# Attention halves, a VectorE split and two stores set elsewhere in a fused linear-attention and FFN kernel

## The chip, the cores and the metric

The kernel runs on one core of one Trainium2 chip. The metric is the device time of one execution in microseconds (us), as the median of several runs.

## The reference

There are 8 batches with 8 heads of 64, and 576 positions in each. Linear attention without a mask is normalised over each head, laid out as 4608 rows of 512, and goes through a feed-forward layer of width 2048:

```python
kv = np.einsum('bhsd,bhse->bhde', k, v)
out = np.einsum('bhsd,bhde->bhse', q, kv)
rms = np.sqrt(np.mean(out * out, axis=-1, keepdims=True) + 1e-06)
x = (out / rms * g_norm).transpose(0, 2, 1, 3).reshape(B * S, H * D)
h = x @ w_in
g = h * (1.0 / (1.0 + np.exp(-h)))
return g @ w_out
```

All is float32. Each operand of a large product is split into a high and a low part, and a product is hi·lo + hi·hi + lo·hi.

## The kernel before

**Tiles.** The rows are 9 tiles of 512 tokens, t = 0 to 8, and the width is 16 blocks of 128, f = 0 to 15. A batch is 576 tokens, so batch 0 fills t=0 and leaves 64 tokens over (class `Rest`, from L390 on), which with most of batch 1 make t=1. Tiles 0 and 1 use plain products: one step is 24 matmuls of 128x256 into an `hp` bank (`products`, L511 through `halves`), a gate, and two steps later 24 matmuls into four `acc` banks (`project`). Tiles 2 to 8 use sums of weight blocks, kept in DRAM (`sums_in_dram`) and loaded again for each pair of blocks (`load_sums`, L676). From t=7 on (`OUT7`) `seven_step` does two blocks at a time.

**The order is written by hand.** Each engine runs its instructions in the order in which the program issues them. A step of t=0 issues:

1. the jobs listed as first for this step;
2. the split of one wo block and one wi block: upper half by a cast on ACT (L215), lower half by a subtraction on POOL (L216);
3. the bit operations of the wo block of this step on DVE (L201, L204, L207), and the magnitude of a wi block four steps ahead on ACT (L181) and POOL (L182);
4. the products of the step on PE ("hp6" in the prediction is that of step 6), and its gate: two activations on ACT (L530, L531) and a subtraction on POOL (L532);
5. the bit operations of a wi block on DVE and the magnitude of a wo block (ACT L181, POOL L182);
6. the jobs listed as mid, the project of the step two back, and the jobs listed as last.

`at_third(n, ...)` puts a job into step n // 3, as first, mid or last by n % 3.

**Batch 1** runs during t=0. `SECOND` (L32) has a row for each of the four pairs of heads: the thirds at which kv and q are split, the first half of out is made, the second half, then its sums and its x. A half (`mm_out`, L314 to L316) is three matmuls into a bank with the tag `at`, 256 columns wide the first time and 320 the second; "p1.0" in the prediction is the first half of pair 1. `copy_out` squares it (ACT L320) and copies it (ACT L321). In t=0 there is one such bank, so a half starts when the one before has been copied. `low_q` (DVE L302) makes the low part of q, `turn_sq` (DVE L325) transposes the squares.

**Buffers.** Five buffers with the tag `tmp` go round in order of allocation: the magnitudes of wi (`full`), the squares and their transpose (`sq`, `sqT`), the scaled rest (`xf`), the results (`ob`) and others. An instruction that writes one waits for the last reader of what was in it.

**The batch-0 rest** goes to x by `x_from`. With `fast` false: scale on ACT into `xf` (L460), cast on ACT (L461), subtraction on POOL (L462). With `fast` true: a scaled cast on ACT from the bank (L451), and scale and subtraction in one DVE operation from the bank (L452).

**Stores.** The results of tile 6 are copied to SBUF in the first two steps of t=7 (`empty`), and each leaves a store of 256 KB in `stores`; the table `between` says at which slot of `seven_step` they are issued. All DMAs of this part are issued by SP, into one queue.

Of the kernel before, what the change touches and what calls it, by code (L numbers as in the profile page):

```python
# [28 lines left out]

SECOND = (13, 17, 18, 20, 39), (17, 19, 21, 24, 40), (19, 22, 24, 27, 44), (22, 25, 28, 30, 41)  # L32


@with_exitstack
def linear_attention_rms_silu_ffn(
# [23 lines left out]
    B, NP, P, S = q.shape  # L60
# [3 lines left out]
    TN = 512  # L64
# [68 lines left out]
    x_second = const.tile([P, NP, 2, TN], F32R, name="x_second")  # L133
# [17 lines left out]
    def block(kind, f, dtype):  # L151
        return weights.tile([P, 2, NP * P], dtype, name=f"{kind}{f}", tag=f"{kind}{f}")
# [101 lines left out]
    class Pair:  # L254
# [101 lines left out]
        def to_tile(self, segment):  # L356
            a, e, t, o = segments(self.b)[segment]
            th, tl = (x_part(t, i, self.c)[:, o:o + e - a] for i in range(2))
            nc.scalar.copy(out=th, in_=self.o[:, a:e])
            nc.gpsimd.tensor_tensor(out=tl, in0=self.o[:, a:e], in1=th.bitcast(F32), op=ALU.subtract)  # L360
# [37 lines left out]
    class Rest:  # L398
# [20 lines left out]
                nc.tensor.transpose(out=self.x[:, w], in_=self.on[:, w], identity=ident)  # L419

        def to_tile(self):
            return x_from([x_second[:, :, a, 0:S - TN] for a in range(2)], self.x.rearrange("d (c n) -> d c n", n=64), False)

    slots = [f"{kind}{f}" for f in range(NF - 1, 0, -1) for kind in ("wo", "wi")]

# [20 lines left out]
    def x_from(tiles, ps, fast):  # L446

        th, tl = tiles
        if fast:
            return [  # L450
                lambda: nc.scalar.activation(out=th, in_=ps, func=AF.Copy, scale=gcol),  # L451
                lambda: nc.vector.scalar_tensor_tensor(  # L452
                    out=tl, in0=ps, scalar=gcol, in1=th.bitcast(F32), op0=ALU.mult, op1=ALU.subtract
                ),
            ]
        full = tmp.tile([P, S], F32, name="xf", tag="tmp")
        a, n = ps.shape[1:]
        full = full[:, :a * n].rearrange("d (a n) -> d a n", n=n)
        return [
            lambda: nc.scalar.activation(out=full, in_=ps, func=AF.Copy, scale=gcol),  # L460
            lambda: nc.scalar.copy(out=th, in_=full),  # L461
            lambda: nc.gpsimd.tensor_tensor(out=tl, in0=full, in1=th.bitcast(F32), op=ALU.subtract),  # L462
        ]
# [29 lines left out]
    def h_bank():  # L493
        return ps_h.tile([P, 512], F32, name="hp", tag="h")
# [51 lines left out]
    emptied, stores = [], []  # L546
# [464 lines left out]
    sevens, queue, between = [], [], {}  # L1011
    W7 = 12, 11, 11, 8

    def open_sevens():

        once["products"], once["seventh"] = h_bank(), h_bank()
        once["forms"] = block("wi", HF + 5, F32)
        once["partial"] = kvq.tile([P, S], F32, name="partial", tag="kvq")[:, :TN].rearrange("p (j n) -> p j n", n=H)
        sevens.extend(Half(h) for h in range(2))
        between.update({(n + 2, "II"): [lambda n=n: load_quarter(OUT7 + 1, n)] for n in range(4)})  # L1020
        for key in ((1, "II"), (1, "III")):
            between[key] = [lambda: stores.pop(0)()] * 2

    def open_gated():

# [4 lines left out]
    def load_quarter(t, n):  # L1030
        row, w = ((0, low), (0, high), (1, high), (1, low))[n]
        nc.sync.dma_start(out=quarter(row, w), in_=x_in_dram[t, row][:, :, w])
# [54 lines left out]
    def seven_step(t, i, groups):  # L1087
# [4 lines left out]
        if opening:  # L1092
            open_sevens()
# [128 lines left out]
    def at_third(n, *calls):  # L1222
        at((first_jobs, mid_jobs, last_jobs)[n % 3], n // 3, *calls)
# [12 lines left out]
    def plan(b, g):  # L1236
# [51 lines left out]
        for p in ps:  # L1288
            half = [lambda p=p, i=i: out_half(p, i) for i in range(2)]
            sums = lambda p=p: p.sum_sq(norms[0][:, p.c])  # L1290
            if b == 1:
                split_at, first_at, second_at, sums_at = SECOND[p.c][:4]
                at_third(split_at, p.split_kv, p.low_kv, p.split_q, p.low_q)
# [34 lines left out]
        for p in ps:  # L1328
            if b == 1:
                n = SECOND[p.c][4]  # L1330
                at_third(n, lambda p=p: p.spread(norms[1][:, p.c], 0), lambda p=p: p.scale(0))
# [6 lines left out]
    with tc.manual_schedule():  # L1338
# [5 lines left out]
        for item in ORDER.split():  # L1344
            kind, n = item.rstrip("0123456789"), int(item.lstrip("wiopbgq") or 0)
# [255 lines left out]
```

## Time and profile before

| what | value |
|---|---|
| runs | 800.72, 800.72, 812.23 us; median 800.72 |
| the profiled execution | 800.1 us, its span 798.3 us |
| granted TensorE clock | 0.998 |
| PE busy | 787.2 us (99%) |
| DVE, ACT, POOL busy | 611.7 (77%), 413.8 (52%), 112.4 us (14%) |
| DMA | 171.08 MB, mean 214 GB/s |

Rows of the timeline read: start, duration, engine, line, operation, out<-in with shapes, count, and in brackets the idle time of the engine before it with what released it. The waits read: engine, output and line that waited, what ended the wait, then total, times and longest in us. Ends of matmuls are modelled, since PE overlaps them; the start of the next matmul says more.

### The profile page before, as it was taken

The page shows a single profiled execution, that of the slowest core. Times are in us where ns is not written, and L with a number is a line of the kernel's source. Part 1 is how long each engine was busy: PE and PEld are TensorE (multiplying, and loading weights), DVE is VectorE, ACT ScalarE, POOL GpSimd, SP SyncE. Part 2 cuts the span into 40 slices and gives each one's busy share as a digit, 9 for nine tenths or more (in the row PEclk, how much of TensorE's full clock was granted, in tenths as well). Part 3 has the DMA queues.
Part 4 walks back from the last instruction along what each step waited for, and adds up shares of the span by engine and source line. Part 5 has one row for each costly group of instructions (what it writes and reads, how often), then busy time and mean ns, then how long its engine had stood idle before and what let it go on. Part 6 is the DMA issues. An engine that isn't in the chain of part 4 may idle for free.

```text
span 798.3 us, 18479 instructions
## 1 busy us (share of the span) xinstructions
PE 787.2 (99%) x7292; PEld 781.2 (98%) x7292; DVE 611.7 (77%) x1328; ACT 413.8 (52%) x871; POOL 112.4 (14%) x116
## 2 busy tenths in 40 slices
PE   8999999999999999999999999999999999999997
PEld 7899999999999999999999999999999999999997
DVE  4999956789779768769878677678867886788666
ACT  4888455445546445635645445445644654465443
POOL 2799781223000000000000000000000000000000
PEclk9999999999999999999999999999999999999999
DMA  9994012743666866766676436976687567657553
GB/s 343 413 413 148 4 61 80 244 157 136 224 236 200 290 218 200 253 215 232 227 256 225 165 107 220 329 250 211 217 252 227 200 225 254 209 201 225 198 186 119
DMA packets 74457, 171.08 MB, mean 214 GB/s; under 512 B 8322, under 2 KB 23170, under 8 KB 74370
## 3 DMA queue, kind: packets, MB, share of 16 engines
q1 hardware_dynamic: 74370, 169.90, 62.4%
q8 instruction: 57, 0.93, 0.5%
q14 instruction: 30, 0.25, 0.1%
HBM read 137.36 MB, written 32.51 MB: 213 GB/s over the span
## 4 chain that ended last, share of the span: by engine, by line
PE 91%; DMA 5%; POOL 2%; issue 1%; DVE 1%; ACT 0%; SPq 0%; DVEq 0%; POOLq 0%
PE hp L747 33%; PE acc L511 26%; PE acc L927 10%; PE hp L511 9%; PE at L927 5%; DMA wo<-in_moe_w_out 3%; PE hp L927 3%; PE at L277 2%; DMA early_wo<-in_q 1%; PE at L314 1%; PE at L315 1%; PE at L316 1%; DMA wi<-sums_in_dram 1%; POOL wo L216 1%; POOL gl L532 0%
## 5 line engine op out<-in xcount | busy, mean ns | idle before, releaser
L511 PE MATMUL acc<-wo,gh 128*128 128x256 f32 x1280 | 200.1, 276 | 0.3 <-POOL wo L216 0.3
L511 PEld LDWEIGHTS acc<-wo,gh 128*128 128x128 f32 x1280 | 170.5, 188 | 0.5 <-POOL wo L216 0.5
L747 PE MATMUL hp<-x_second,wi 128*128 128x256 f32 x1152 | 153.4, 277 | 0.0
L747 PEld LDWEIGHTS hp<-x_second,wi 128*128 128x128 f32 x1152 | 141.1, 188 | 0.3
L511 PE MATMUL acc<-wo,gl 128*128 128x256 f32 x640 | 124.6, 276 | 0.0
L747 PE MATMUL hp<-operand,wi 128*128 128x256 f32 x912 | 120.9, 276 | 0.6 <-DMA wi<-sums_in_dram 0.4
L747 PEld LDWEIGHTS hp<-operand,wi 128*128 128x128 f32 x912 | 111.3, 188 | 1.0 <-DMA wi<-sums_in_dram 0.6
L511 PEld LDWEIGHTS acc<-wo,gl 128*128 128x128 f32 x640 | 96.3, 188 | 0.0
L873 ACT ACTIVATE wi<-wi 128x512 f32<-128x512 f32 x64 | 40.5, 633 | 97.5 <-DVE wi L1181 75.0
L978 POOL TENSOR_TENSOR e<-e,partial 128x256 f32<-128x256 f32 x2 | 1.5, 733 | 592.3 <-DVE e L978 592.3
L927 PE MATMUL acc<-wo,gh 128*128 128x256 f32 x256 | 46.8, 276 | 0.0
L511 PE MATMUL hp<-x_second,wi 128*128 128x256 f32 x384 | 46.3, 277 | 0.0
L511 PE MATMUL hp<-x,wi 128*128 128x256 f32 x360 | 44.5, 278 | 0.7 <-POOL x L462 0.7
L511 PEld LDWEIGHTS hp<-x_second,wi 128*128 128x128 f32 x384 | 45.0, 188 | 0.1
L511 PEld LDWEIGHTS hp<-x,wi 128*128 128x128 f32 x360 | 42.4, 188 | 1.1 <-POOL x L462 0.9
L927 PE MATMUL acc<-s,gs 128*128 128x256 f32 x288 | 43.0, 276 | 0.0
L320 ACT ACTIVATE sq<-at 128x256 f32<-128x256 f32 (+1 forms) x56 | 22.9, 409 | 36.1 <-PE at L316 29.8
L1181 DVE TENSOR_TENSOR wi<-hp,partial 128x256 f32<-128x256 f32 x32 | 13.6, 425 | 35.9 <-PE hp L747 35.9
L927 PEld LDWEIGHTS acc<-wo,gh 128*128 128x128 f32 x256 | 38.6, 188 | 0.0
L927 PEld LDWEIGHTS acc<-s,gs 128*128 128x128 f32 x288 | 37.4, 188 | 0.0
L1166 ACT COPY wi<-hp 128x256 f32<-128x256 f32 x32 | 11.9, 373 | 48.4 <-PE hp L747 48.4
L747 PE MATMUL hp<-moved,wi 128*128 128x256 f32 x288 | 36.8, 277 | 0.0
(207 smaller groups left out, 1660.8 us busy)
## 6 DMA issues: line engine op xcount, KB each, us to landing
wi<-sums_in_dram SPq DMA_DIRECT2D x112, 512.0 KB, 3.8
s<-out_sums SPq DMA_DIRECT2D x96, 256.0 KB, 4.7
wi<-in_moe_w_in SPq DMA_DIRECT2D x16, 512.0 KB, 8.1
wo<-in_moe_w_out SPq DMA_DIRECT2D x16, 512.0 KB, 9.0
sums_in_dram<-sum_parts SPq DMA_DIRECT2D x16, 512.0 KB, 2.9
out_sums<-wi SPq DMA_DIRECT2D x16, 512.0 KB, 3.0
k<-in_k SPq DMA_DIRECT2D x28, 288.0 KB, 4.3
v<-in_v SPq DMA_DIRECT2D x28, 288.0 KB, 4.6
```

What stands on the lines that cost most here:

```text
L216: nc.gpsimd.tensor_tensor(out=w[:, 1, :], in0=full, in1=w[:, 0, :].bitcast(F32), op=ALU.subtract)
L277: nc.tensor.matmul(out=self.kv[h], lhsT=self.k[rows, c, :], rhs=self.v[rows, c, :], start=(start and r == 0), stop=(stop and r == 4),)
L314: nc.tensor.matmul(out=ps, lhsT=self.kh, rhs=self.ql[:, w], start=True, stop=False)
L315: nc.tensor.matmul(out=ps, lhsT=self.kl, rhs=self.qh[:, w], start=False, stop=False)
L316: nc.tensor.matmul(out=ps, lhsT=self.kh, rhs=self.qh[:, w], start=False, stop=True)
L320: nc.scalar.activation(out=self.sq[:, self.w], in_=self.ps, func=AF.Square)
L511: nc.tensor.matmul(out=to[:, at:at + 256], lhsT=stationary, rhs=moving[:, at:at + 256], start=start and at == 0, stop=stop and at == n - 256,)
L747: nc.tensor.matmul(out=out, lhsT=a_of(i, a, c), rhs=x[b][:, c], start=start and n == 0, stop=n == 5, skip_group_check=not check,)
L873: nc.scalar.activation(out=self.gated, in_=self.gated, func=AF.Silu)
L927: nc.tensor.matmul(out=self.out[m], lhsT=g[m], rhs=self.weight(m, j, a), start=j == 0 and n == 0 and m in self.opens, stop=j == HF - 1 and ...
L1166: nc.scalar.copy(out=first.gated[:, low], in_=u)
L1181: nc.vector.tensor_tensor(out=first.gated[:, high], in0=u, in1=u3, op=ALU.add)
```

## The change

Three edits:

- Seven numbers of `SECOND` are a third higher: the second half of pair 0 (18 to 19, from first to mid in step 6) and its sums (20 to 21), both halves of pair 1 (19 to 20, 21 to 22) and of pair 2 (22 to 23, 24 to 25), and the first half of pair 3 (25 to 26). All others stay, the second half of pair 3 (28) and the sums of pairs 1 to 3 too.
- `Rest.to_tile` passes True.
- Of the four stores, two stay at slot II of step 1 of tile 7, and two go from slot III of step 1 to slot II of step 2, ahead of what is listed there.

```diff
-SECOND = (13, 17, 18, 20, 39), (17, 19, 21, 24, 40), (19, 22, 24, 27, 44), (22, 25, 28, 30, 41)
+SECOND = (13, 17, 19, 21, 39), (17, 20, 22, 24, 40), (19, 23, 25, 27, 44), (22, 26, 28, 30, 41)
...
         def to_tile(self):
-            return x_from([x_second[:, :, a, 0:S - TN] for a in range(2)], self.x.rearrange("d (c n) -> d c n", n=64), False)
+            return x_from([x_second[:, :, a, 0:S - TN] for a in range(2)], self.x.rearrange("d (c n) -> d c n", n=64), True)
...
         between.update({(n + 2, "II"): [lambda n=n: load_quarter(OUT7 + 1, n)] for n in range(4)})
-        for key in ((1, "II"), (1, "III")):
-            between[key] = [lambda: stores.pop(0)()] * 2
+        for key in ((1, "II"), (2, "II")):
+            between.setdefault(key, [])[:0] = [lambda: stores.pop(0)()] * 2
```

**ACT, step 7 of t=0**, before (`full` and `wo_full` are magnitudes of a wi and a wo block, `wi` and `wo` the split blocks, `gh` and `gf` the gate, `sq` and `o` the copy of a half; the brackets name whose progress the instruction waits for):

```order
L215 CAST wo_1059<-wo_full 128x512 [waits DVE_49]
L215 CAST wi_1062<-full 128x512 [waits DVE_49]
L181 ACTIVATE full<-wi_231 128x512 [waits DMAHW1_49,DVE_49]
L530 ACTIVATE gh<-hp 128x512 [waits PE_49]
L531 ACTIVATE gf<-hp 128x512 [waits Pool_49]
L181 ACTIVATE wo_full<-wo_229 128x512 [waits DMAHW0_49,Pool_49]
L320 ACTIVATE sq<-at 128x256 [waits DVE_49,PE_49]
L321 COPY o<-at 128x256
L290 CAST kh<-kvm 128x128
```

In the changed kernel:

```order
L215 CAST wo_1051<-wo_full 128x512 [waits DVE_49]
L215 CAST wi_1054<-full 128x512 [waits DVE_49]
L181 ACTIVATE full<-wi_231 128x512 [waits DMAHW1_49,Pool_49]
L530 ACTIVATE gh<-hp 128x512 [waits PE_49]
L531 ACTIVATE gf<-hp 128x512
L181 ACTIVATE wo_full<-wo_229 128x512 [waits DMAHW0_49]
L320 ACTIVATE sq<-at 128x320 [waits PE_49]
L321 COPY o<-at 128x320
L290 CAST kh<-kvm 128x128
```

The 128x320 copy, which belongs to pair 1 in both, was made ahead of the step's casts (it is the two rows above the first fence) and is now behind wo_full. The magnitude full<-wi_231 waits for POOL where it waited for DVE; the next two rows that waited for POOL don't name it any more. In step 8 the row full<-wi_239 changes in the same way.

**PE, steps 5 and 6 of t=0** (`at` is a half of pair 0, `hp<-x_404,wi_...` the first products of step 6, with three more blocks of x behind them), before and in the changed kernel:

```order
L314 MATMUL at<-ql,kh 128x256
L315 MATMUL at<-qh,kl 128x256
L316 MATMUL at<-qh,kh 128x256
L314 MATMUL at<-ql,kh 128x320
L315 MATMUL at<-qh,kl 128x320
L316 MATMUL at<-qh,kh 128x320
L511 MATMUL hp<-x_404,wi_783 128x256 x4
```

```order
L314 MATMUL at<-ql,kh 128x256
L315 MATMUL at<-qh,kl 128x256
L316 MATMUL at<-qh,kh 128x256
L511 MATMUL hp<-x_404,wi_781 128x256 x4
...
L314 MATMUL at<-ql,kh 128x320
L315 MATMUL at<-qh,kl 128x320
L316 MATMUL at<-qh,kh 128x320
```

The second half of pair 0 has moved behind the products. The halves of pairs 1 and 2 and the first of pair 3 have each moved behind the next group of 24 matmuls in the same way: p1.0, p2.0 and p3.0 from ahead of a project to behind it, p1.1 and p2.1 from ahead of a step's products to behind them.

**SP, from step 1 of tile 7** (`out<-ob` are the stores, `wi<-sums_in_dram` the weight sums of a step's half, `s` and `wo` output sums, `x_in_dram<-o` and `x<-x_in_dram` the x of later tiles), before:

```order
L676 DMA wi_3090<-sums_in_dram 128x1024
L554 DMA out<-ob 128x512 x4
L676 DMA wi_3092<-sums_in_dram 128x1024
L1009 DMA wo_657<-out_sums 128x2x256
L1009 DMA s<-out_sums 128x512 x3
L354 DMA x_in_dram<-o 128x64
L354 DMA x_in_dram<-o 128x512
L676 DMA wi_3090<-sums_in_dram 128x1024
L1032 DMA x_0_1941<-x_in_dram 128x2x256
```

And in the changed kernel:

```order
L676 DMA wi_3088<-sums_in_dram 128x1024
L554 DMA out<-ob 128x512 x2
L676 DMA wi_3090<-sums_in_dram 128x1024
L1009 DMA wo_655<-out_sums 128x2x256
L1009 DMA s<-out_sums 128x512 x3
L354 DMA x_in_dram<-o 128x64
L354 DMA x_in_dram<-o 128x512
L676 DMA wi_3088<-sums_in_dram 128x1024
L554 DMA out<-ob 128x512 x2
L1032 DMA x_0_1939<-x_in_dram 128x2x256
```

Two stores have moved behind two loads of weight sums; the second of these is the load issued at 505.39 in the profiled execution.

## The prediction

> **What bounds the kernel now.** First the busy shares, then the waits of PE, then the two stretches of 20 us in which the changed instructions lie (columns: busy time and instructions of PE, PEld, DVE, ACT, POOL, then granted clock, DMA share, GB/s).
>
> ```profile
> PE 787.2 (99%) x7292; PEld 781.2 (98%) x7292; DVE 611.7 (77%) x1328; ACT 413.8 (52%) x871; POOL 112.4 (14%) x116
> ...
> PE at L314 <- ACT o L321: 0.7, 1, 0.7
> PE hp L747 <- DMA wi<-sums_in_dram: 0.4, 1, 0.4
> PE acc L511 <- POOL wo L216: 0.3, 1, 0.3
> ...
> 40.00:60.00 20.00, 19.27 (x224) 18.80 (x224) 18.63 (x28) 17.60 (x41) 19.83 (x20) 1.00 1.03 413
> 60.00:80.00 20.00, 20.00 (x176) 20.00 (x175) 19.35 (x30) 16.03 (x36) 18.05 (x19) 1.00 0.47 147
> ```
>
> PE sets the time: it idles 798.3 − 787.2 = 11.1 us in all, at the full clock. No scheduling edit can win more than that, and what makes PE late here is late for good, since no later slack gives it back. The three waits listed are the ones that the three edits touch, one each. The windows show a second thing that the average of 14% hides: from 40 to 60 POOL is busy 19.83 of 20 us, DVE 18.63 and ACT 17.60. While t=0 splits its weights, four engines run nearly full, and a copy on ACT can be had late, not free.
>
> **The batch-0 rest on VectorE.** The chain around it:
>
> ```profile
> 35.25 0.62 ACT L215 CAST wo<-wo_full 128x512 fp32r<-128x512 f32 x1
> 35.72 0.74 POOL L462 TENSOR_TENSOR x_second<-xf,x_second 128x256 fp32r<-128x256 f32 x1
> 36.42 1.30 POOL L216 TENSOR_TENSOR wo<-wo_full,wo 128x512 fp32r<-128x512 f32 x1
> 36.88 0.39 PE L511 MATMUL acc<-wo,gh 128*128 128x256 f32 x2
> 37.77 0.74 PE L511 MATMUL acc<-wo,gh 128*128 128x256 f32 x4 [0.28 <-POOL wo L216]
> 40.25 2.70 PE L277 MATMUL at<-v,k 128*64 128x64 f32 x80
> ```
>
> POOL's lower half of wo1 ends at 37.72 and PE starts with it at 37.77. Without L462 ahead, L216 starts when the upper cast ends, about 35.9, and ends at 37.2. A project is 24 matmuls of 128x256, which take 2.72 without a stall (55.67 to 58.39 in the next fence but one), so it would end at 36.88 + 2.72 = 39.60 instead of 40.25: **gain 0.65**. The 0.28 shown is smaller, since matmul ends are modelled and the refill of the pipe lies in their durations. The ACT side is neutral or better, one cast (L451) in place of two operations.
>
> DVE gets one L452 of 128x256. Nearest row: a subtraction of the same shape from the same bank, 0.42 below, behind which the next operation starts after 0.34. So it takes 0.34 of DVE's queue, at most 0.42.
>
> ```profile
> 26.93 0.42 DVE L441 TENSOR_TENSOR on<-at,y 128x256 f32<-128x256 f32 x1
> 27.27 0.68 DVE L201 TENSOR_SCALAR conv<-wo_full 128x512 int32<-128x512 int32 x1
> ...
> 46.80 0.69 DVE L201 TENSOR_SCALAR conv<-wo_full 128x512 int32<-128x512 int32 x1 [0.47 <-POOL wo_full L182]
> ```
>
> DVE's own idle 0.47 at 46.80 takes that up, but the bits made before it are late, so ACT's cast and POOL's L216 at 46.94 are too. From there on POOL has next to no gap (19.83 of 20.00 above): I count POOL 0.34 later up to its next idle time (63.44, below).
>
> **Pair 0's halves apart.** PE order before: p0.0, p0.1, hp6 (the 24 products of step 6). After: p0.0, hp6, p0.1.
>
> ```profile
> 53.88 0.28 PE L314 MATMUL at<-ql,kh 128*128 128x256 f32 x1
> 54.70 0.37 ACT L321 COPY o<-at 128x256 f32<-128x256 f32 x1
> 55.12 0.42 PE L314 MATMUL at<-ql,kh 128*128 128x320 f32 x1 [0.73 <-ACT o L321]
> 55.67 2.88 PE L511 MATMUL hp<-x,wi 128*128 128x256 f32 x24
> 58.39 0.28 PE L314 MATMUL at<-ql,kh 128*128 128x256 f32 x1
> ```
>
> There is one "at" bank in t=0, so p0.1 waits until ACT has copied p0.0. The two halves stream in 0.34 (three matmuls of 0.113 each) and 0.42 (in the ratio of 320 to 256 columns), so hp6 could start at 53.88 + 0.77 = 54.65 and starts at 55.67. With hp6 between, the copy at 54.70 lies under products: **gain 1.02**. PE is now 1.67 ahead.
>
> **What is late next.** The same rule now binds at three other places. Before, p1.0 stands ahead of project and p1.1 behind it, so the copy of p1.0 lies under 2.72 us of project. After, p0.1, p1.1 and p2.1 stand directly ahead of a project and p1.0, p2.0 and p3.0 directly behind it, so that each copy has a project to hide under; but on ACT it sits behind a wi magnitude, both gates and a wo magnitude (order rows of ACT). Place by place, with the time at which PE would want the half in bold:
>
> p1.0: PE runs p0.0 at 53.23, hp6 to 56.29, p0.1, project to **59.44**.
>
> ```profile
> 57.47 1.80 POOL L216 TENSOR_TENSOR wo<-wo_full,wo 128x512 fp32r<-128x512 f32 x1
> 59.56 0.68 ACT L181 ACTIVATE wo_full<-wo 128x512 f32<-128x512 f32 x1
> 60.40 0.39 ACT L321 COPY o<-at 128x256 f32<-128x256 f32 x1
> 61.45 0.30 PE L314 MATMUL at<-ql,kh 128*128 128x320 f32 x1
> ```
>
> The magnitude L181 of wo7 needs the buffer that this L216 frees, at 59.27 + 0.34 = 59.61. From L181's start to the end of the copy went 60.79 − 59.56 = 1.23, and 0.1 more for 320 columns: copy done at 60.95, p1.0 at 61.0. That is a stall of 1.57, and 0.12 for refilling the pipe (at 511.88, in a later fence, six matmuls take 0.97 after a stall and 0.84 without one): **1.69**. It eats the 1.67 gained.
>
> p2.0: hp7 from 61.47, p1.1, project to **67.34**.
>
> ```profile
> 63.44 1.35 POOL L216 TENSOR_TENSOR wo<-wo_full,wo 128x512 fp32r<-128x512 f32 x1 [0.42 <-ACT wo L215]
> 64.75 1.29 POOL L216 TENSOR_TENSOR wi<-full,wi 128x512 fp32r<-128x512 f32 x1
> 64.35 0.68 ACT L181 ACTIVATE full<-wi 128x512 f32<-128x512 f32 x1 [0.47 <-DVE sqT L325]
> 64.93 0.57 ACT L530 ACTIVATE gh<-hp 128x512 fp32r<-128x512 f32 x1
> 65.41 0.58 ACT L531 ACTIVATE gf<-hp 128x512 f32<-128x512 f32 x1
> 65.89 0.68 ACT L181 ACTIVATE wo_full<-wo 128x512 f32<-128x512 f32 x1
> ```
>
> The magnitude of wi11 (64.35) waits for a buffer. It has waited for DVE's transpose of the squares; without the xf buffer, and with the squares allocated later, the five buffers rotate otherwise, and in the order rows it waits for POOL. Two later rows of the same step no longer wait for POOL (L531 and wo8's L181 did, for work older than wi9's), so what wi11 waits for must lie behind theirs: the L216 of wi9 (64.75). That ends at 65.95 in my walk: wi11 at 65.98, gates and wo8's magnitude 1.54 later (65.89 − 64.35) at 67.52, copy done 1.33 behind, 68.85. p2.0 at 68.90: 1.56 + 0.12 = **1.68**.
>
> p3.0: hp8 from 69.36, p2.1, project to **75.23**.
>
> ```profile
> 69.47 0.63 ACT L215 CAST wi<-full 128x512 fp32r<-128x512 f32 x1
> 70.92 0.68 ACT L181 ACTIVATE full<-wi 128x512 f32<-128x512 f32 x1 [0.82 <-DVE sqT L325]
> 71.32 1.31 POOL L216 TENSOR_TENSOR wi<-full,wi 128x512 fp32r<-128x512 f32 x1
> 73.91 2.88 PE L511 MATMUL hp<-x,wi 128*128 128x256 f32 x24
> ```
>
> The same with wi12 and wi10: ACT's casts stand behind the copy of p2.0, so wi10's comes at 70.68 instead of 69.47, its L216 ends at 73.45 instead of 72.63, wi12's magnitude starts at 73.48 instead of 70.92, and the copy of p2.1 is done at 73.48 + 1.54 + 1.33 = 76.35. p3.0 at 76.38: 1.15 + 0.12 = **1.27**. Then hp9, which has the same work ahead of it in both orders, starts at 76.84 instead of 73.91. From there the orders agree: together **+4.6**.
>
> [...]
>
> **Two stores a step later.**
>
> ```profile
> 496.29 3.07 SPq L554 DMA_DIRECT2D out<-ob  x4
> 505.39 0.32 SPq L676 DMA_DIRECT2D wi<-sums_in_dram  x1
> 510.64 0.84 PE L747 MATMUL hp<-operand,wi 128*128 128x256 f32 x6
> 511.88 0.97 PE L747 MATMUL hp<-operand,wi 128*128 128x256 f32 x6 [0.41 <-DMA wi<-sums_in_dram]
> ...
> 515.60 0.32 SPq L676 DMA_DIRECT2D wi<-sums_in_dram  x1
> ...
> 506.00:508.00 2.00, 2.00 (x20) 2.00 (x19) 0.95 (x2) 0.00 (x0) 0.00 (x0) 1.00 1.05 392
> ```
>
> The seventh matmul wants its weights at 510.64 + 6 × 0.113 = 511.32 and starts at 511.88; with the refill (0.97 against 0.84) 0.69 is lost. The queue is full (DMA share 1.05). Two stores of 256 KB behind this load instead of ahead of it take 512 KB / 392 GB/s = 1.3 us off its landing, if its wait is one of bandwidth: **gain 0.69**. Between nothing and 0.69 I take all, since 1.3 is twice the need. The 1.3 us of the stores now lie ahead of the load issued at 515.60, which stands in the next step as the one at 505.39 does in this: if it came as late, up to 0.69 would come back there. I take none, as ten microseconds lie between them and it. SP passes a store in 3.07 / 4 = 0.8 us, which that queue has.
>
> **Sum**, on the profiled execution of 800.1 (span 798.3 and 1.8 around it): −0.65 − 1.02 + 4.6 − 0.69 = **+2.25**, 802.3. The median of the runs is 0.6 above that execution: 800.72 + 2.25 = **803.0 us**, +0.3%. A measurement of this kernel tells about 2% from no change, so that reads as no change.
>
> **Rivals.**
> 1. The copies come in time: the buffers that the magnitudes wait for are free early and ACT, 52% busy over all, runs the copies under project. Only the gains stay: −0.65 − 1.02 − 0.69 = −2.36, 798.4, which is not slower. For it: the waits removed are real. Against: POOL's 19.83 of 20.00, ACT's 17.60 of 20.00, and in the order rows the magnitudes ahead of each copy.
> 2. The wait on wi9 and wi10's L216 doesn't bite and ACT is paced by DVE as before (64.35, 70.92): the copy of p1.1 is done at 64.35 + 1.54 + 1.33 = 67.2, no stall over 0.4 at p2.0, as little at p3.0. Stalls 1.69 + 0.8 instead of 4.6: about +0.1, 800.8. For it: the transposes also come later, so that the two could nearly tie. Against: the order rows name POOL alone.
> 3. POOL is slower than in the walk: L216 of wo6, wi9, wo7 and wi10 next to DVE's ql, each 1.80 instead of 1.30. Decided by whether ql2 and ql3 run inside these operations: +0.5 to +2.0 at PE, with +1.5 804.5.
> 4. The stores do nothing for the load (its 6 us are its own latency): 0.69 less gain, 803.7; it joins with any of these.
>
> **Chances.** Forecast 0.5 (801.8 to 804), rival 1 0.12, rival 2 0.2, rival 3 0.13, rival 4 alone 0.05. The range 798.4 to 804.8 leaves out half of rival 1 and the end of rival 3, and holds the bounds of L452 (0.34 to 0.42) and of the stores (0 to 0.69). Faster by over 2% would need 16 us where PE idles 11.1: 0.01. Slower by over 2% needs a wait that none of these rows shows, 0.02. Within 2%: 0.97.
>
> **What would show it.** In the waits of PE, the ones on L321 at 55.12, on L216 at 37.77 and on sums_in_dram at 511.88 are gone; three new ones "PE at L314 <- ACT o L321" of 1.1 to 1.6 each stand near 61, 69 and 76. ACT's L181 of wi11 and wi12 waits for POOL L216. hp9 starts near 76.8. PE busy stays at 787 and the clock at 1.00. I am wrong if ACT's copies end before project does (rivals 1 and 2), or if PE's waits on L321 add up to over 6 (rival 3).

## The result, and the profile after

| | before | changed |
|---|---|---|
| median of the runs | 800.72 us | 804.28 us (803.15 to 805.49, 5 runs) |
| ratio to before, 95% interval | | 1.0052 [1.0035, 1.0069] |
| profiled execution, span | 800.1, 798.3 us | 805.49, 803.7 us |

The changed kernel is 0.5% slower, clear of its interval: 3.6 us where the prediction had 2.25. In the runs below some executions of most kernels, the kernel before among them, take about 10 us more, and the ratios leave out only a part of these, so that an interval of half a percent either way cannot show a gain of 1 us, and the traces are compared by the stretch from the start of p0.0 to the start of hp9 wherever that can be done.

Two things told ahead are not so. `OUT7` is 5, so the stretch with the four stores belongs to tile 5 and the stored rows to tile 4, not to 7 and 6; the times and rows quoted there are the right ones. And the buffers rotate otherwise with `SECOND` alone; the missing `xf` is not needed for it (first experiment).

Busy shares, the waits of PE and the two stretches in the changed kernel:

```profile
PE 789.0 (98%) x7292; PEld 782.7 (97%) x7292; DVE 613.8 (76%) x1329; ACT 413.1 (51%) x870; POOL 111.8 (14%) x115
...
PE at L314 <- ACT o L321: 3.7, 3, 2.3
...
PE hp L747 <- DMA wi<-sums_in_dram: 0.8, 1, 0.8
...
40.00:60.00 20.00, 19.86 (x230) 19.53 (x228) 18.89 (x26) 17.22 (x41) 19.62 (x20) 1.00 1.03 413
60.00:80.00 20.00, 16.39 (x136) 16.00 (x137) 16.86 (x26) 12.27 (x29) 14.88 (x15) 1.00 0.37 118
```

From 40 to 60 PE is busier (19.86 for 19.27): the stall at 55.12 is gone, as is the one at 37.77, ahead of this window. From 60 to 80 it falls from 20.00 to 16.39, with three waits on L321 in place of one. PE's total is nearly the same, 789 for 787 us. The wait for weight sums is still there, and twice as long. Where PE stands (timeline of the changed kernel):

```profile
53.47 0.28 PE L314 MATMUL at<-ql,kh 128*128 128x256 f32 x1
...
53.81 2.88 PE L511 MATMUL hp<-x,wi 128*128 128x256 f32 x24
...
56.53 0.30 PE L314 MATMUL at<-ql,kh 128*128 128x320 f32 x1
...
60.47 0.38 PE L314 MATMUL at<-ql,kh 128*128 128x256 f32 x1 [0.61 <-ACT o L321]
...
69.26 0.39 PE L314 MATMUL at<-ql,kh 128*128 128x256 f32 x1 [2.27 <-ACT o L321]
...
76.64 0.38 PE L314 MATMUL at<-ql,kh 128*128 128x256 f32 x1 [0.86 <-ACT o L321]
...
77.10 2.99 PE L511 MATMUL hp<-x,wi 128*128 128x256 f32 x24
```

hp6 follows p0.0 at once, and then p1.0, p2.0 and p3.0 each wait for the copy of the half before. hp9 starts at 77.10, 3.19 later than before (73.91). From p0.0 to hp9 it is 23.63 us, before 73.91 − 53.88 = 20.03: **+3.60**. That this equals the difference of the medians is in part luck: the stretch leaves out the 0.41 that the rest's edit wins ahead of p0.0 (53.47 for 53.88). The 3.19 at hp9 is what these edits come to in the trace; the other 0.4 of the medians is not placed.

Why the copies are late, on POOL, DVE and ACT:

```profile
57.59 1.32 POOL L216 TENSOR_TENSOR wo<-wo_full,wo 128x512 fp32r<-128x512 f32 x1
57.69 1.84 DVE L302 TENSOR_TENSOR ql<-q,qh 128x576 fp32r<-128x576 f32 x1
...
58.88 1.80 POOL L216 TENSOR_TENSOR wi<-full,wi 128x512 fp32r<-128x512 f32 x1
59.10 0.68 ACT L181 ACTIVATE wo_full<-wo 128x512 f32<-128x512 f32 x1
59.98 0.43 ACT L321 COPY o<-at 128x320 f32<-128x320 f32 x1
...
64.50 1.83 POOL L216 TENSOR_TENSOR wi<-full,wi 128x512 fp32r<-128x512 f32 x1
66.37 0.67 ACT L181 ACTIVATE full<-wi 128x512 f32<-128x512 f32 x1 [1.94 <-DMA k<-in_k]
...
67.90 0.66 ACT L181 ACTIVATE wo_full<-wo 128x512 f32<-128x512 f32 x1
68.76 0.44 ACT L321 COPY o<-at 128x320 f32<-128x320 f32 x1
...
73.74 0.69 ACT L181 ACTIVATE full<-wi 128x512 f32<-128x512 f32 x1 [2.14 <-POOL wi L216]
```

The magnitude of wi11 starts at 66.37, when POOL's L216 of wi9 has ended (64.50 + 1.83 = 66.33). The bracket names a DMA, which only happened to end last among what the wait could be matched with; in second_only and late_wo_only, below, the same wait is put down to POOL L216. Gates, wo8's magnitude and the copy follow, and the copy ends at 69.20, just ahead of p2.0. At p3.0 it is the same with wi12's magnitude (73.74), which waits 2.14 for L216. At p1.0 it is not: wo7's magnitude starts at 59.10 with no wait that the row shows, and the copy at 59.98 is late by what stands ahead of it on ACT, not by a buffer.

### The profile page after: what moved, and what is told of

It is laid out like the page before. It is cut to its first block, busy times and chain, and to the rows that moved or that the text cites. A ratio compares the mean times of both kernels' runs of the same rounds, so it can differ in the third digit from the quotient of the medians.

```text
span 803.7 us, 18472 instructions
## 1 busy us (share of the span) xinstructions
PE 789.0 (98%) x7292; PEld 782.7 (97%) x7292; DVE 613.8 (76%) x1329; ACT 413.1 (51%) x870; POOL 111.8 (14%) x115
## 4 chain that ended last, share of the span: by engine, by line
PE 89%; DMA 4%; DVE 3%; ACT 1%; issue 1%; POOL 1%; SPq 0%; DVEq 0%; POOLq 0%
PE hp L747 33%; PE acc L511 25%; PE acc L927 10%; PE hp L511 8%; PE at L927 5%; PE hp L927 3%; PE at L277 2%; DMA k<-in_k 1%; PE at L314 1%; DMA wi<-in_moe_w_in 1%; DVE conv L204 1%; DMA wi<-sums_in_dram 1%; DMA early_wi<-in_q 1%; PE at L315 1%; PE at L316 1%
## 5 line engine op out<-in xcount | busy, mean ns | idle before, releaser
L320 ACT ACTIVATE sq<-at 128x256 f32<-128x256 f32 (+1 forms) x56 | 22.9, 409 | 36.2 <-PE at L316 30.0
```

The costliest lines, as they stand in the source:

```text
L320: nc.scalar.activation(out=self.sq[:, self.w], in_=self.ps, func=AF.Square)
```

## The experiments

**One part alone.** Three kernels, each with one of the three hunks of the change.

`second_only`: the line of `SECOND`. 

> Only the seven numbers of SECOND; the rest stays with POOL, the stores stay. Theory (copies late on ACT, behind magnitudes that wait for POOL): gain 1.02 at pair 0, three stalls of together 4.6 at p1.0, p2.0 and p3.0, the wi11 magnitude waiting for POOL L216 as in the changed kernel: +3.6 us, 804.3. Rival (the buffers moved because the rest no longer takes one, and POOL was late through the rest's edit): stalls of at most 2.5, +1.5 us or less, 802.2.

Measured: ratio 1.0047 [1.0032, 1.0062], 803.7 us. Its waits of PE and of ACT (46 to 80 us):

```profile
PE at L314 <- ACT o L321: 3.2, 2, 2.4
...
PE at L314 <- DVE ql L302: 0.4, 1, 0.4
```

```profile
ACT full L181 <- POOL wi L216: 3.5, 2, 2.1
```

From p0.0 to hp9 it takes 23.69 us, as in the whole change. So the seven numbers make the whole loss, and the two magnitudes wait for L216, 3.5 us in all. The rest's buffer isn't needed for it; that point of the prediction falls. Here p1.0 waits 0.4, and for ql; in the whole change it waits 0.61 for the copy, so in these two traces the rest's edit, which wins 0.41 ahead of p0.0, costs 0.2 there.

`rest_only`: the line of `Rest.to_tile`. 

> Only the rest of batch 0 split on VectorE. Theory (POOL paces the copies in t=0): the 0.4 won at L216 of wo1 is lost again at p0.1, whose bank is copied behind a magnitude that waits for POOL; PE's wait on L321 grows from 0.7 to 1.1 or 1.3: 0.0 to +0.2 us, 800.7 to 800.9. Rival (the gain stays): -0.4 to -0.65 us, 800.1 to 800.3.

Measured: ratio 1.0004 [0.9955, 1.0053], which can't tell −0.4 from 0. The trace does: p0.1 waits longer.

```profile
57.24 0.41 PE L314 MATMUL at<-ql,kh 128*128 128x320 f32 x1 [1.22 <-ACT o L321]
```

Against 0.73 before, the wait has grown by 0.49, all of the 0.4 won at L216. Alone, this edit brings nothing that this trace shows. It is one trace, in which PE had also waited 1.4 us for a DMA ahead of p0.0.

`stores_only`: the two lines on `between`. 

> Only the two stores a step later. The prediction's term: the wait for weight sums at 511.88 goes, -0.69 us, 800.0. Rival, from the trace of the changed kernel (its wait there is 0.82, not 0.41): the stores ahead of the load cost it nothing, and with two behind it it lands no earlier or later: 0 to +0.4 us, 800.7 to 801.1, with a wait of 0.4 to 0.8 at the same place.

Measured: ratio 1.0021 [0.9975, 1.0067], which can't tell −0.69 us from 0; the wait is still there, with 0.2.

**Is it the buffer, or the queue on ACT?** `sums_later` leaves the order of the copies and moves the sums of the squares a third on, which changes what buffer each magnitude gets (the edit is against the changed kernel):

```diff
-SECOND = (13, 17, 19, 21, 39), (17, 20, 22, 24, 40), (19, 23, 25, 27, 44), (22, 26, 28, 30, 41)
+SECOND = (13, 17, 19, 22, 39), (17, 20, 22, 25, 40), (19, 23, 25, 28, 44), (22, 26, 28, 31, 41)
```

> The whole change, and the sums of the squares of all four pairs another third later (21, 24, 27, 30 to 22, 25, 28, 31), so that wi11's magnitude gets the buffer of wi8, free long before, and wi12's one that DVE frees; the order of the copies on ACT is the same. Theory (the buffer that waits for L216 of wi9 and wi10 is the largest part): the stall at p2.0 falls from 2.3 to under 0.7 and the one at p3.0 falls or stays: 2 us less than the changed kernel, 802.3. Rival (ACT is late by its queue alone, whatever the buffer): stalls as in the changed kernel, 804.0 or more.

Measured: 805.4 us, ratio 1.0103 [1.0036, 1.0169]; no faster than the changed kernel (804.28), where 2 us less was expected. The timeline of PE and of ACT:

```profile
66.93 0.38 PE L314 MATMUL at<-ql,kh 128*128 128x256 f32 x1
...
80.15 0.41 PE L314 MATMUL at<-ql,kh 128*128 128x320 f32 x1 [2.25 <-ACT o L321]
```

```profile
64.02 0.67 ACT L181 ACTIVATE full<-wi 128x512 f32<-128x512 f32 x1
...
79.45 0.38 ACT L320 ACTIVATE sq<-at 128x256 f32<-128x256 f32 x1 [5.06 <-DVE sqT L325]
```

The part that was tested came out as the theory had it: wi11's magnitude starts at 64.02 instead of 66.37, and p2.0 at 66.93 has no wait left that the row shows. The total did not: the later sums free the squares' own buffers later, ACT's L320 waits 5.06 us for a transposition, and p3.1 stalls in place of p2.0. With five buffers, a later reader moves the wait to whoever draws that buffer next.

**The order on ACT.** `late_magnitudes` is the whole change, with the magnitudes of steps 6 to 8 issued behind the copy:

```diff
+LATE = (6, 7, 8)
...
-                if t == 0 and f + 4 < NF:
+                if t == 0 and f + 4 < NF and f not in LATE:
                     magnitude("wi", f + 4)
...
-                if t == 0 and f + 1 < NF:
+                if t == 0 and f + 1 < NF and f not in LATE:
                     magnitude("wo", f + 1)
                 for job in mid_jobs.pop(g, ()):
                     job()
+                if t == 0 and f in LATE:
+                    magnitude("wi", f + 4)
+                    magnitude("wo", f + 1)
```

> The whole change; in steps 6 to 8 of t=0 the two magnitudes are issued behind the copy of the half, so ACT makes gate, copy, magnitudes. Theory (a copy is late for what stands ahead of it on ACT): the copies of p0.1 and p1.1 come within 0.2 us of the end of project, the stall at p2.0 goes from 2.3 to under 0.3; at p3.0 up to 1.0 stays, since the cast of wi10 still stands ahead of the gate and waits for DVE: 3 us less than the changed kernel, 801.0, or 0 to +0.5 us against the kernel before. Rival (DVE and POOL pace the step whatever ACT's order): stalls of together 3 us or more, 803.5 or more.

Measured: 799.8 us, ratio 0.9963 [0.992, 1.0005]. One wait on L321 is left, at p3.0:

```profile
65.42 0.38 PE L314 MATMUL at<-ql,kh 128*128 128x256 f32 x1
...
72.55 0.39 PE L314 MATMUL at<-ql,kh 128*128 128x256 f32 x1 [0.62 <-ACT o L321]
73.01 2.88 PE L511 MATMUL hp<-x,wi 128*128 128x256 f32 x24
```

p0.0 starts at 52.89 in this trace, so p0.0 to hp9 is 20.12 us, 3.5 less than in the changed kernel, with the same instructions on every engine.

`late_splits` puts the casts and lower halves behind the copy as well, ahead of the magnitudes:

```diff
-                for item in prepped:
-                    split_block(*item, nc.scalar.copy)
+                splits = [lambda item=item: split_block(*item, nc.scalar.copy) for item in prepped]
+                if not (t == 0 and f in LATE):
+                    run(splits)
...
                 if t == 0 and f in LATE:
+                    run(splits)
                     magnitude("wi", f + 4)
```

> As late_magnitudes, and the upper casts and lower halves of step 6 to 8 are issued behind the copy too: gate, copy, casts, magnitudes. Theory: no wait on L321 over 0.2 us at any of the three places, the gains of 0.4 and 1.0 stay: -1.4 us against the kernel before, less or more by up to 0.7 for the load of weight sums, 798.5 where before is 799.9. Rival (a project or a DVE operation waits for the later casts): new waits of PE on L215 or L216 of 1 us or more, 800.5 or more.

Measured: 799.2 us, ratio 0.9968 [0.9919, 1.0017], and once more 

> late_splits once more: no wait on L321 at all, 4 to 5 us less than the changed kernel and 0.7 to 1.5 us less than the kernel before.

799.0 us, ratio 0.9935 [0.9886, 0.9985]. No wait on L321 in either; the second trace:

```profile
53.87 0.28 PE L314 MATMUL at<-ql,kh 128*128 128x256 f32 x1
54.21 2.88 PE L511 MATMUL hp<-x,wi 128*128 128x256 f32 x24
...
72.89 2.88 PE L511 MATMUL hp<-x,wi 128*128 128x256 f32 x24
```

p0.0 to hp9 is 19.02 us in both, 1.01 less than the 20.03 of before. That is the gain that the change was open to at pair 0, whole, once nothing on ACT is late. In the first run its median is 1.0 us below that of the kernel before (800.25), where 1.4 was expected; one of its two intervals excludes no change and the other doesn't, so it is the stretch that shows the gain.

**Which magnitude.** One of the two moved behind the copy, the other left ahead, one execution each. The rows are p1.0, p2.0 and p3.0 of the first, p1.0 and p2.0 of the second.

`late_wi_only`: 

> The whole change with only the wi magnitude of steps 6 to 8 behind the copy; the wo magnitude stays ahead of it. Theory (most of the stall at p2.0 is the wi11 magnitude, which waits for a buffer that POOL's L216 of wi9 frees): PE's stall at p2.0 falls from 2.3 to 0.5 or less, at p3.0 about 1 stays; hp9 starts 1.5 to 2 us earlier than in the changed kernel (77.1). Rival (two magnitudes of 0.5 to 0.7 us in the queue, both alike): 0.6 off each stall, hp9 about 1.2 us earlier, and the same for the wo magnitude alone.

```profile
61.26 0.38 PE L314 MATMUL at<-ql,kh 128*128 128x256 f32 x1 [0.51 <-ACT o L321]
...
67.81 0.28 PE L314 MATMUL at<-ql,kh 128*128 128x256 f32 x1
...
74.78 0.38 PE L314 MATMUL at<-ql,kh 128*128 128x256 f32 x1 [0.37 <-ACT o L321]
```

`late_wo_only`: 

> The whole change with only the wo magnitude of steps 6 to 8 behind the copy. Theory: the stall at p2.0 only loses the magnitude's own 0.5, from 2.3 to 1.8, and so at the others; hp9 about 1 us earlier than in the changed kernel. Rival (queue alone): as much as for the wi magnitude alone.

```profile
59.50 0.38 PE L314 MATMUL at<-ql,kh 128*128 128x256 f32 x1
...
68.30 0.38 PE L314 MATMUL at<-ql,kh 128*128 128x256 f32 x1 [2.30 <-ACT o L321]
68.75 4.45 PE L511 MATMUL hp<-x,wi 128*128 128x256 f32 x24
```

With wi's magnitude out of the way the stall at p2.0 is gone; with wo's alone it stays, 2.30 for 2.27. It is the wait inside wi11's magnitude that makes this stall, not the length of the queue; even the 0.5 that the theory gave to wo's was too much. At p1.0 it is the other way round: 0.51 of the stall is left with wi's magnitude behind the copy, and no wait that the row shows with wo's. So both matter, each at its own place. The start of hp9 misses its expectation for the first (from p0.0 at 54.36 to hp9 at 75.24 it is 20.88 us, 2.75 less than in the changed kernel, where 1.5 to 2 was expected) and can't be read for the second, since its clock fell to 0.50 (last section).

**The stores.** `late_splits_old_stores` has the stores where they were, `no_stores` is the kernel before without them (the 512 rows of tile 4's result are not written), and `after_again` is the changed kernel once more.

> As late_splits, with the four stores where they were. If the stores' place decides the wait for weight sums, PE's wait near 510 is 0.4 or more here and absent in late_splits (the prediction's view: 0.7 us slower than late_splits); if that wait comes and goes with other transfers, it is 0 to 0.8 in both without a rule, and the two agree within 0.5 us.

> The kernel before without the four stores (512 rows of the output of tile 4 are not written): bounds what any place of them can bring. Prediction's view: the queue is 1 MB shorter ahead of the load, the wait for weight sums at 511.9 is gone, -0.7 us. Rival (the load is late by the traffic of the s and wo loads ahead of it): a wait of 0.2 to 0.8 stays, 0 us within 0.3.

> The changed kernel once more, beside late_splits. Theory: three waits on L321 as in its first trace, of together 3 to 4 us; +3 to +4 us against the kernel before. The wait for weight sums near 517 was 0.8 the first time; if it hangs on other transfers and not on where the stores stand, it differs now by 0.3 or more.

The row of waits leaves out the shortest ones. The twelve matmuls that need this load take 1.36 from the start of the first to the start of what follows when nothing is late, so what they take above 1.36 is what the load costs. In the changed kernel, in its repeat and without stores (the row behind the twelve is the one that follows):

```profile
515.35 0.84 PE L747 MATMUL hp<-operand,wi 128*128 128x256 f32 x6
517.01 0.97 PE L747 MATMUL hp<-operand,wi 128*128 128x256 f32 x6 [0.82 <-DMA wi<-sums_in_dram]
517.81 0.39 PE L927 MATMUL at<-wo,gh 128*128 128x256 f32 x2
```

```profile
514.53 1.52 PE L747 MATMUL hp<-operand,wi 128*128 128x256 f32 x12
515.89 0.39 PE L927 MATMUL at<-wo,gh 128*128 128x256 f32 x2
```

```profile
510.89 1.75 PE L747 MATMUL hp<-operand,wi 128*128 128x256 f32 x12
512.49 0.40 PE L927 MATMUL at<-wo,gh 128*128 128x256 f32 x2
```

That is 1.1, 0 and 0.2. So read, one trace of each kernel:

| stores | lost at the load, us |
|---|---|
| four at once (as before) | 0.7 (before), 0 (second_only), 0.3 (rest_only), 0.6 (late_splits_old_stores) |
| two and two (changed) | 1.1 (changed), 0 (after_again), 0.5 (stores_only), 0.6 (sums_later), 0.2 (late_magnitudes), 0 (late_splits), 0 (its repeat), 0.4 (late_wi_only), 0.2 (late_wo_only) |
| none | 0.2 (no_stores) |

The same program loses 1.1 in one execution and nothing in another. late_splits_old_stores against late_splits (0.6 against 0) would by itself speak for the stores' place; the changed kernel against second_only (1.1 against 0) speaks against it. No rule by the stores' place comes out of these traces, the loss is there without any store too, and leaving the stores out brings no time (ratio 1.0024 [0.9977, 1.0072]). late_splits_old_stores came to 0.9987 [0.993, 1.0043], too wide to tell it from late_splits (its quickest execution, 797.3 us, is the quickest of the case); its p0.0 to hp9 is 19.02 as well. after_again repeats the three stalls (its row of waits is the first one's, to a tenth) at a ratio of 1.0032 [0.9984, 1.008], with p0.0 to hp9 at 23.59.

## Why the prediction was right and wrong

- **Mechanism: right, with one of its waits wrong.** Three waits on L321 at 60.5, 69.3 and 76.6 were predicted at 61, 69 and 76, and the copies are late for what stands ahead of them on ACT, as late_magnitudes and late_splits show. At p2.0 and p3.0 the magnitudes of wi11 and wi12 wait for POOL's L216 of wi9 and wi10, as forecast. At p1.0 the forecast had wo7's magnitude wait for L216 until 59.61; it starts at 59.10 without that wait, and the queue on ACT makes the stall.
- **The stalls' sum: right, by luck in part; their sizes not.** In the timeline of the changed kernel the projects ahead of the three halves begin at 56.97, 64.09 and 72.88 and take 2.72; the halves start 0.78, 2.45 and 1.04 after that, where 1.57, 1.56 and 1.15 were forecast: 4.27 against 4.28 before the refills. p1.0 came out low since PE came 0.25 later than forecast and the copy 0.54 earlier: L216 of wo5 got in ahead of ql (57.59 and 57.69) and took 1.32, not 1.80; then ql took 1.84 instead of 1.17, and the next L216 1.80. p2.0 came out high since PE, less delayed at p1.0, came 0.53 earlier, and since L216 of wi9 took 1.83, not 1.29, and ended at 66.33, not 65.95. That is the third rival's mechanism, which bit at one of its four places: wi9's L216 started 0.06 behind ql (64.44, 0.75) and took 1.83, where those of wo6, wo7 and wi10 took 1.29, 1.30 and 1.29. In the first pair, with POOL 0.1 ahead, the operations trade places: L216 of wo5 gains 0.48, ql loses 0.67, and the next L216, which starts while ql runs, loses 0.50. In the kernel before, ql was 0.53 ahead of L216 of wo5, and L216 took 1.80:

```profile
56.94 1.17 DVE L302 TENSOR_TENSOR ql<-q,qh 128x576 fp32r<-128x576 f32 x1
...
57.47 1.80 POOL L216 TENSOR_TENSOR wo<-wo_full,wo 128x512 fp32r<-128x512 f32 x1
```

  In each of these pairs the operation that started second took longer than the median of its line in its trace (1.80 and 1.83 for 1.30 at L216, 1.84 for 0.75 at ql); why, no run shows.
- **Pair 0's halves: right.** 1.02 was forecast; late_splits shows 1.01.
- **The stores: wrong, and the step that failed.** The term of −0.69 rested on "512 KB / 392 GB/s = 1.3 us off its landing, if its wait is one of bandwidth" and took all of a range from nothing to 0.69. In its place the runs show no gain: the changed kernel lost 1.1 at that load in one execution and nothing in another, where the kernel before had lost 0.7, and stores_only and no_stores still lose 0.5 and 0.2. One execution's wait of 0.41 was read as a property of the program. The runs can't tell a gain of 0.69 in the total from none.
- **The rest: mis-sized.** 0.65 was forecast from the start of the next matmul group. L216 of wo1 ended the stall, but PE's matmul after it went from 37.77 to 37.36, 0.41 earlier:

```profile
36.01 1.29 POOL L216 TENSOR_TENSOR wo<-wo_full,wo 128x512 fp32r<-128x512 f32 x1 [0.25 <-ACT wo L215]
...
37.31 0.48 DVE L452 SCALAR_TENSOR_TENSOR x_second<-at,gcol,x_second 128x256 fp32r<-128x256 f32 x1
37.36 0.73 PE L511 MATMUL acc<-wo,gh 128*128 128x256 f32 x4
```

  The kv products follow at 39.84 instead of 40.25, the same 0.41; the other 0.24 of the forecast is time that PE takes there in both kernels. L452 took 0.48, and the next operation followed after 0.40, where 0.34 was taken; POOL, counted 0.34 later, was 0.12 later at L216 of wo5 (57.59 for 57.47).
- **The sum.** With 0 for the stores and 0.41 for the rest, the prediction's own terms give 2.25 + 0.69 + 0.24 = +3.2 us. That is the 3.19 by which hp9 is later in the trace; beside the 3.6 of the medians 0.4 stays open.
- **"Reads as no change": wrong.** The text took 2% as what the measurement can tell. The interval of this comparison was 0.17% either way, so +0.5% is told from no change, and the forecast of +0.3% would have been too.

## What to carry to other kernels

When a half or tile is moved to hide its copy, follow the copy too: list what the program puts ahead of it on the copying engine, and which of those instructions waits for a buffer. Here the same move loses 3.6 us or wins 1 over the stretch from p0.0 to hp9, by whether the casts and the two magnitudes stand ahead of the copy or behind it. And a DMA wait of a few tenths that is seen in one execution needs a second one before anything is built on it; the last section shows that more than its length may hang on it.

## What the runs showed of the hardware

**The clock after a stall.** In late_wo_only the 24 matmuls behind the stall at p2.0 take 4.45 instead of 2.88, with the granted clock at half (windows of it; the clock is the third number from the end):

```profile
66.00:68.00 2.00, 0.00 (x1) 0.00 (x0) 1.93 (x4) 2.00 (x5) 0.93 (x2) 1.00 0.55 162
68.00:70.00 2.00, 1.70 (x13) 1.70 (x14) 1.90 (x4) 2.00 (x7) 1.30 (x2) 0.93 0.00 0
70.00:72.00 2.00, 2.00 (x11) 2.00 (x11) 0.50 (x1) 1.15 (x3) 1.56 (x3) 0.50 0.00 0
72.00:74.00 2.00, 2.00 (x14) 2.00 (x14) 0.37 (x2) 0.74 (x2) 1.23 (x1) 0.71 0.00 0
```

The same happens in sums_later around p3.1, behind a stall of 2.25 us: the granted clock is 0.77, 0.50 and 0.88 in the windows 80:82, 82:84 and 84:86. In the changed kernel a stall of the same length (2.27 us) costs no clock: it is 1.00 in every window of 2 us from 66 to 74. What decides whether the clock falls, these runs don't show.

**Matmuls 4% slower at the full clock.** hp9 of the changed kernel takes 2.99 where hp6 of the same trace takes 2.88, with the granted clock at 1.00 in both. In the changed kernel's trace there are two such stretches of 20 to 26 us, from 76 and from 200: 24 products take 2.99 at 94.64 and 2.88 at 100.19, then 2.90 at 197.63 and 2.99 at 204.16 and 209.81, and four matmuls of a project 0.63 at 224.74 and 0.62 at 226.22. They are where the profiled execution loses more behind hp9: the matmul that is 3.19 later at hp9 (77.10 for 73.91) is 4.71 later at the weight sums (515.35 for 510.64), with no longer wait in between.

In five traces (rest_only, stores_only, no_stores, sums_later, late_wi_only) such a stretch begins right behind the loss at the weight sums, at 512 to 518, and lasts nearly to the end: in rest_only six products take 0.84 at 512.48, ahead of it, and 0.87 at 517.11, in stores_only 0.84 at 510.36 and 0.87 at 513.67. Windows of no_stores ahead of it and behind it:

```profile
490.00:510.00 20.00, 20.00 (x179) 20.00 (x179) 15.36 (x36) 10.24 (x21) 0.00 (x0) 1.00 0.77 250
520.00:540.00 20.00, 20.00 (x172) 20.00 (x171) 14.05 (x34) 7.93 (x16) 0.00 (x0) 1.00 0.73 239
```

PE makes 172 matmuls in 20 us where it made 179, at a granted clock of 1.00 (late_magnitudes makes 179 in both windows). Over the 280 us that are left, 4% are about 11 us (an estimate from these rows), and the five executions took 810 to 817 us. Of the other nine traces, which took 799 to 806 us, four lose nothing at that load and five lose 0.2 to 1.1, and in none does such a stretch begin there. So a loss of a few tenths at this load goes with ten microseconds in some executions. Whether it sets them off, and what else is needed, stays open; the stores are not needed, since no_stores has it too.
